# The diagonal of the first ten units summed by the tensor engine, and the weight work of a recurrent-attention kernel re-placed

## The chip, the cores and the metric

The kernel runs on one core of one Trainium2 chip. The metric is the device time of one launch in microseconds (us); smaller is better. The engines are called by their short names: PE (tensor engine, with its weight loads as PEld), DVE (vector engine), ACT (scalar engine), POOL (GpSimd) and SP (which only issues DMAs here).

## The reference

Three stages follow each other, in fp32; sizes are B=4, H=8, S=768, D=48 for the first, D_FF=1024 for the second, E=4 experts of head size 64 for the third.

```python
# stage 1: a recurrence over time with a decay w and a "bonus" u for the current step
for t in range(S):
    kt, vt, rt, wt = (k[:, :, t], v[:, :, t], r[:, :, t], w[:, :, t])
    cur = np.einsum('bhd,bhe->bhde', u[None] * kt, vt)
    y[:, :, t] = np.einsum('bhd,bhde->bhe', rt, state + cur)
    state = wt[:, :, :, None] * state + np.einsum('bhd,bhe->bhde', kt, vt)
# stage 2: x (4, 768, 384) -> relu(x @ w_in) -> conv over 3 steps -> h * sigmoid(conv) @ w_out
# stage 3: four causal softmax attentions on the result, mixed by a top-2 gate, output (4, 768, 384)
```

Only stage 1 and the weights of stage 2 are touched here. In stage 1 the bonus gives each time step one number per head, the sum over the 48 channels of r * u * k; it stands on the diagonal of the matrix that multiplies v.

## The kernel before

**Units and slots.** Stage 1 is cut into 32 units: a batch, a half of the sequence (three chunks of 128 steps) and a pair of heads, 2 x 48 channels padded to 2 x 64 partitions. `slot(u)` is written out 33 times in program order, and each engine works through its own instructions in the order in which the slots issue them. A slot finishes unit u, prepares unit u + 1, puts out unit u - 1, and from slot 5 on also carries one or two "groups" of stage 2 (a group is 128 of the 1024 hidden channels over one half of one batch). The slots are told apart below by DVE's first scan in them (L205, tile `Dp`), so "slot 3" runs from the L205 of slot 3 to that of slot 4.

**One unit.** `scan_d` and `scan_f` (L205, L212) are running products of the decay along time, `K` and `Q` (L215, L220) multiply k and r with them. `trans` turns K's chunks with PE (L266) and copies them out with ACT (`KT`, L268); `scores` is K times Q (L252), `state` KT times v (L278). `bonus` multiplies r, k and u on POOL (L225, L226), in a layout with time on the partitions (`rn`, `kn` of the `rkv` load), `diag` sums that over channels on DVE (L231, tile `e`) and spreads it on the diagonals of `AT` with two affine selects on POOL (L234). `masked` copies the scores below the diagonal into AT (L258, DVE). `carry` folds the state into the running states `Ss` (L289, L292, DVE). `yout` multiplies AT and the states out (L306, L312), `rows` splits the result in a high and a low part (ACT L324, DVE L325). `check` tests the decay's range on ACT (L243).

**PSUM.** `trans`, `state` and `yout` take their results in turn from one pool of two buffers (`ps_m`, name "m"), so `trans` of a unit gets the buffer that `carry` of the unit before it has read (L289). The hidden tile `hs` of a group has one buffer, which the ACT copy `ht` (L354) frees.

**Weights.** The weights of stage 2 arrive as float64 and are rebuilt from their words in eight pieces of 128 x 768, in slots 2 to 9 before the change: `conv1_w` masks and shifts on DVE (L75, L76), makes the low part on ACT (L72) and adds on POOL (L77); for the four `win` pieces `conv2_w` then rounds on ACT (L173) and takes the remainder on POOL (L174). In slots 10 to 17 the eight pieces are loaded again and `check_w` tests them on ACT (L185, L186).

**Stage 2 in a slot.** `mlp1` (L350), the ACT copies `ht` and `ct` (L354, L358), `conv` on DVE (L369 and L371, or L373 and L374) with a tanh on ACT (`st`, L377), `gate` on DVE (L387), and four groups later `mlp2` (L400).

Of the kernel before, what the change touches and what calls it, by code (L numbers as in the profile page):

```python
# [23 lines left out]
C = 128  # L24
# [63 lines left out]
def phase1(tc, nc, a, x2, ident, stat, lim, top, right, left2):  # L88
# [88 lines left out]

# [214 lines left out]
    def mlp2(g):  # L392
# [9 lines left out]
        if f == NF - 1:  # L402
# [23 lines left out]
    def slot(u):  # L426

        ga = 2 * u - G0
        s1u, nxt = u < 2 * NU, u + 1 < 2 * NU
        for i, (z, n, m) in enumerate(WS):  # L430
            if u == z - 2:
                load_w(n, m)
        if s1u:
            trans(u)
        conv(ga - 1)
        if nxt:
            bonus(u + 1)
# [25 lines left out]
        for i, (z, n, m) in enumerate(WS):  # L463
            if u == z:
                (conv2_w if i < 8 else check_w)(n, m)
        if u == 1:
            conv_w()
        if u == 18:
            rawc.close()
        groups(ga + 1)  # L470
        if u + 3 < 2 * NU:
            load(u + 3)

    with tc.manual_schedule(engines=mine):
        bonus(0)
# [643 lines left out]
```

## Time and profile before

| what | value |
|---|---|
| median of 3 runs | 658.96 us (657.47 to 659.04) |
| the profiled execution, its own time | 659.13 us |
| its span | 657.4 us |
| PE, DVE, ACT, POOL busy in the span | 586.6, 517.6, 347.9, 183.2 us |

The span is what the profiler saw from the first to the last instruction; the other 1.7 us lie around it. "Busy" counts an instruction from start to end, and a DVE instruction that is held up after its start counts as busy as well. A row of the timeline gives start, duration, engine, line, operation, what it writes and reads, shapes, and in brackets how long the engine had been idle before it and who ended that. Several instructions of one kind in a row are drawn together (x3).

### The profile page before, as it was taken

To read this page: it belongs to the slowest core of one execution; us is meant where nothing else is said; L and a number is where in the kernel's file an instruction comes from. 1 tells how busy PE (TensorE), PEld (TensorE's weight loads), DVE (VectorE), ACT (ScalarE), POOL (GpSimd) and SP (SyncE) were. 2 spreads that over 40 slices of the span, in tenths; PEclk is the share of its full clock that TensorE was granted. 3 is DMA by queue.
4 is the path that set the end of the run, shared out by engine and by line. 5 is a ranking of instruction groups with operands and counts; after the bars stand their busy time and mean duration, and the time that the engine had idled before them with its cause. 6 is when DMAs were issued, how large, how long until landed. Compare 5 with 4: busy or idle time off the path is not lost.

```text
span 657.4 us, 11247 instructions
## 1 busy us (share of the span) xinstructions
PE 586.6 (89%) x3978; PEld 464.9 (71%) x3978; DVE 517.6 (79%) x1151; ACT 347.9 (53%) x819; POOL 183.2 (28%) x245
## 2 busy tenths in 40 slices
PE   2665689799999999999999999989997999799896
PEld 1553567577676777777777776968786987788754
DVE  6999999988888999999995643688765876776471
ACT  3233444566666545556355552666654665556452
POOL 6478444222222233224321710030002002102260
PEclk9957789989999999999999999999998999999999
DMA  8655445475774455454513652265036514442502
GB/s 315 214 162 208 171 151 178 147 230 179 219 215 135 126 165 158 133 169 134 160 59 96 173 139 67 85 170 144 25 90 175 145 37 128 126 98 84 133 1 77
DMA packets 34401, 92.39 MB, mean 141 GB/s; under 512 B 5024, under 2 KB 14368, under 8 KB 34336
## 3 DMA queue, kind: packets, MB, share of 16 engines
q1 hardware_dynamic: 34336, 91.59, 46.7%
q8 instruction: 33, 0.54, 0.3%
q14 instruction: 32, 0.26, 0.1%
HBM read 53.77 MB, written 9.44 MB: 96 GB/s over the span
## 4 chain that ended last, share of the span: by engine, by line
PE 48%; DVE 29%; ACT 9%; DMA 7%; issue 4%; SPq 2%; POOL 1%; ACTq 0%; DVEq 0%; POOLq 0%
PE x L400 9%; PE hs L350 7%; PE m L767 6%; PE st L841 5%; PE m L891 5%; PE t L875 4%; DVE Fp L212 4%; PE m L903 4%; PE m L797 3%; DVE Dp L205 3%; DMA x<-x 2%; DVE AT L258 2%; DVE wm L76 2%; DVE ct L374 2%; DVE ct L369 2%
## 5 line engine op out<-in xcount | busy, mean ns | idle before, releaser
L400 PE MATMUL x<-gt,wout 128*128 128x386 f32 (+1 forms) x384 | 135.0, 490 | 0.0
L350 PE MATMUL hs<-X,win 128*128 128x384 f32 (+1 forms) x576 | 121.7, 357 | 8.2 <-ACT ht L354 8.1
L350 PEld LDWEIGHTS hs<-X,win 128*128 128x128 f32 x576 | 101.1, 193 | 17.6 <-ACT ht L354 11.7
L377 ACT ACTIVATE st<-ct 128x382 f32<-128x382 f32 (+1 forms) x64 | 33.6, 525 | 126.3 <-DVE ct L371 67.4
L400 PEld LDWEIGHTS x<-gt,wout 128*128 128x128 f32 x384 | 73.0, 192 | 35.8 <-issue 1.2
L855 ACT ACTIVATE A<-sm,mn 128x128 f32<-128x128 f32 (+5 forms) x96 | 63.8, 665 | 28.3 <-DVE mn L854 27.5
L854 DVE CUSTOM_DVE_ANT_0 sm<-st,mask 128x128 f32<-128x128 f32 (+5 forms) x96 | 58.3, 619 | 20.8 <-PE st L841 18.2
L234 POOL TENSOR_SCALAR_AFFINE_SELECT AT<-e 128x384 f32<-128x384 f32 x64 | 32.4, 531 | 141.8 <-DVE e L231 134.2
L875 PE MATMUL t<-ident,A 128*128 128x128 f32 x336 | 53.5, 276 | 2.1 <-ACT T L879 1.2
L266 PE MATMUL m<-ident,K 128*128 128x128 f32 x80 | 16.6, 312 | 36.6 <-DVE Ss L289 26.4
L841 PE MATMUL st<-sk,sq 128*128 128x384 f32 (+3 forms) x128 | 44.8, 360 | 2.7 <-DVE mn L854 1.8
L753 POOL TENSOR_TENSOR xs<-x,xs 128x768 fp32r<-128x768 f32 x12 | 22.4, 1884 | 88.8 <-ACT xs L752 88.8
L881 DVE COPY T<-t 128x128 f32<-128x128 f32 (+3 forms) x64 | 32.2, 504 | 18.4 <-PE t L875 17.9
L387 DVE SCALAR_TENSOR_TENSOR gt<-st,ht 128x382 f32<-128x382 f32 (+1 forms) x64 | 38.1, 596 | 10.9 <-ACT st L377 7.9
L841 PE MATMUL st<-sl,sq 128*128 128x384 f32 (+3 forms) x128 | 41.1, 334 | 5.8 <-DMA sl<-kl 5.8
L875 PEld LDWEIGHTS t<-ident,A 128*128 128x128 f32 x336 | 40.3, 140 | 8.4 <-issue 2.2
L252 PEld LDWEIGHTS sc<-Q,K 64*128 64x128 f32 x384 | 30.7, 218 | 20.5 <-issue 5.6
L266 PEld LDWEIGHTS m<-ident,K 128*128 128x128 f32 x80 | 11.0, 156 | 46.8 <-DVE Ss L289 29.8
L891 PE MATMUL m<-T,V 128*64 128x384 f32 (+2 forms) x288 | 43.8, 422 | 0.0
L879 ACT ACTIVATE T<-t 128x512 f32<-128x512 f32 (+3 forms) x64 | 28.6, 447 | 25.4 <-PE t L875 20.6
L252 PE MATMUL sc<-Q,K 64*128 64x128 f32 x384 | 37.6, 325 | 4.2 <-DVE AT L258 4.2
L358 ACT ACTIVATE ct<-ht,cwk 128x382 f32<-128x382 f32 (+1 forms) x64 | 39.5, 617 | 2.0
(126 smaller groups left out, 1216.2 us busy)
## 6 DMA issues: line engine op xcount, KB each, us to landing
wkr<-in_wkr SPq DMA_DIRECT2D x32, 578.0 KB, 3.8
rkv<-in_rkv SPq DMA_DIRECT2D x32, 480.0 KB, 4.5
rawt<-in_win SPq DMA_DIRECT2D x8, 768.0 KB, 5.5
rawt<-in_wout SPq DMA_DIRECT2D x8, 768.0 KB, 5.2
sk<-kh SPq DMA_DIRECT2D x32, 192.0 KB, 3.3
sl<-kl SPq DMA_DIRECT2D x32, 192.0 KB, 4.0
x<-x SPq DMA_DIRECT2D x12, 384.0 KB, 3.9
out_dram<-ot SPq DMA_DIRECT2D x24, 192.0 KB, 1.9
```

The lines of the kernel that those rows point to most:

```text
L252: nc.tensor.matmul(sc[j][:, c], t["K"][p, c], t["Q"][p, c], start=True, stop=True)
L350: nc.tensor.matmul(hs[:, 0:N], win[wi][:, f // 2, i, (f % 2) * 128:(f % 2 + 1) * 128], x[:, i, xi], start=(n == 0), stop=(n == 8))
L358: nc.scalar.activation(ct, ht[:, o:o + N], AF.Copy, scale=w[:, 1, f:f + 1])
L377: nc.scalar.activation(st, ct, AF.Tanh)
L387: nc.vector.scalar_tensor_tensor(gt, st, 1.0, ht[:, o:o + N], op0=OP.add, op1=OP.mult)
L400: nc.tensor.matmul(acc[0][i][:, 0:N], wout[:, f, i * 128:(i + 1) * 128], gt, start=(f == 0), stop=(f == NF - 1))
L767: nc.tensor.matmul(pt[:, 0:HT], w[wi][:, i, p * 128:(p + 1) * 128], xs[xi][:, i, s], start=(m == 0), stop=(m == 8))
L841: nc.tensor.matmul(st[:, z, 0:n], q[:, qi * C:(qi + 1) * C], k[:, z * n:(z + 1) * n], start=(i == 0), stop=(i == 1))
L854: nc.vector.tensor_tensor_reduce(o3, i3, m3, 1.0, 3e38, op0=OP.add, op1=OP.min, accum_out=mn)
L855: nc.scalar.activation(at, o3, AF.Exp, bias=mn, scale=-1.0, accum_out=rs[:, qi % 3:qi % 3 + 1])
L875: nc.tensor.transpose(pt[:, ki - k0], at[:, ki * C:(ki + 1) * C], self.ident)
L891: nc.tensor.matmul(po[o, lo:HT], V[:, ki, (2 * p + j) * 64:(2 * p + j + 1) * 64], Ts[j][:, ki, lo:], start=(ki == 0), stop=(ki == n - 1))
```

## The change

For units 0 to 9 (`BONUS_ON_PE = 10`) the two POOL products and the DVE sum go. DVE multiplies k by r in place, in the layout with channels on the partitions (`diag`, a 128 x 384 product), and in the next slot's `trans` PE multiplies each of the three chunks with a 2-column matrix `u_c`, which holds u of the pair of heads and zeros; ACT copies the 128 x 6 result to `e`, and the affine selects follow there. The r and k of these units in the other layout are no longer loaded (192 instead of 480 KB). `u_c` is loaded by two DMAs of single 4-byte elements, ahead of the loads of units 1 and 2.

The weight work is placed anew: the pieces are loaded one slot before their use, `conv1_w` stands at the end of slots 1 to 8, ahead of `masked`, and `conv2_w` at the head of the slot after, with its subtraction on DVE instead of POOL. `check` goes from behind the second conv to behind the first group, `check_w` from the slot's end to ahead of `scores`, `carry` from ahead of `masked` to behind `rows`, and the small `conv_w` from slot 1 to slot 0.

```diff
+        zn = 2 * CH * 64 if u < BONUS_ON_PE else NRKV
+        nc.sync.dma_start(z[:, 0:zn], a["rkv"][q, h][:, 0:zn])
+    u_c = cst.tile([128, HP, 2], F32, name="u_c")
+    nc.gpsimd.memset(u_c, 0.0)
+    for j in range(2):
+        nc.sync.dma_start(u_c[64 * j:64 * j + D, :, j],
+                          bass.AP(tensor=a["u"].tensor, offset=a["u"].offset + j * D, ap=[[1, D], [2 * D, HP]]))
...
-        nc.gpsimd.tensor_tensor(d1, t, _f(d0), op=OP.subtract)
+        nc.vector.tensor_tensor(d1, t, _f(d0), op=OP.subtract)
...
     def diag(u):
         t = T[u]
-        e = wk.tile([128, 2, CH], F32, name="e")
+        if u < BONUS_ON_PE:
+            nc.vector.tensor_tensor(t["k"], t["k"], t["r"], op=OP.mult)
+            return
+        e = t["e"] = wk.tile([128, 2, CH], F32, name="e")
         nc.vector.tensor_reduce(e, t["rn"], axis=AX.X, op=OP.add)
+        blocks(u)
...
+        if u < BONUS_ON_PE:
+            es = m[:, CH * 128:].rearrange("p (j c) -> p j c", j=2)
+            for c in range(CH):
+                nc.tensor.matmul(es[:, :, c], t["k"][:, c], u_c[:, hp], start=True, stop=True)
+            e = t["e"] = wk.tile([128, 2, CH], F32, name="e")
+            nc.scalar.activation(e, es, AF.Copy)
+            blocks(u)
         nc.scalar.activation(KT[:, 0:n], kt[:, 0:n], AF.Copy)
...
         if nxt:
-            bonus(u + 1)
+            if u + 1 >= BONUS_ON_PE:
+                bonus(u + 1)
             scan_d(u + 1)
-        for i, (z, n, m) in enumerate(WS[0:8]):
-            if u == z:
-                conv1_w(n, m)
+        for z, n, m in WS:
+            if u == z + 1:
+                conv2_w(n, m)
         gate(ga - 1)
         groups(ga)
+        if s1u:
+            check(u)
...
         gate(ga)
+        for z, n, m in WC2:
+            if u == z:
+                check_w(n, m)
         if s1u:
-            check(u)
             scores(u)
             state(u)
...
             diag(u + 1)
+        for z, n, m in WS:
+            if u == z:
+                conv1_w(n, m)
         if s1u:
-            carry(u)
             masked(u)
         if 0 < u <= 2 * NU:
             rows(u - 1)
-        for i, (z, n, m) in enumerate(WS):
-            if u == z:
-                (conv2_w if i < 8 else check_w)(n, m)
-        if u == 1:
+        if s1u:
+            carry(u)
+        if u == 0:
             conv_w()
```

In the changed file the lines stand 8 to 23 further down, so the scan `Dp` is L213 there, and so on. The order of DVE's instructions in slot 3 was this (`wm` is the rebuilt weight piece, `wkr` the load with w, k and r):

```order
L205 SCALAR_TENSOR_TENSOR Dp<-wkr,cD 128x387
L75 TENSOR_SCALAR wm<-rawt 128x768
L76 SCALAR_TENSOR_TENSOR wm<-rawt,wm 128x768
L210 RECIPROCAL cF<-Dp 128x3
L212 SCALAR_TENSOR_TENSOR Fp<-wkr,cF 128x387
L215 TENSOR_TENSOR K<-wkr,Fp 128x384
L220 TENSOR_TENSOR Q<-wkr,Dp 128x384
L231 TENSOR_REDUCE e<-rkv 128x6
L289 TENSOR_TENSOR Ss_128<-m,Dp 128x3x48
L292 SCALAR_TENSOR_TENSOR Ss_128<-Ss_128,Dp 128x48 x2
L258 COPY_PREDICATED AT<-msk,sc 128x384 x2
L325 TENSOR_TENSOR Y<-m,Y 128x384
```

The same slot on DVE after the change, with `win_143` the remainder of the piece before:

```order
L213 SCALAR_TENSOR_TENSOR Dp<-wkr,cD 128x387
L182 TENSOR_TENSOR win_143<-wm,win_142 128x768
L218 RECIPROCAL cF<-Dp 128x3
L220 SCALAR_TENSOR_TENSOR Fp<-wkr,cF 128x387
L223 TENSOR_TENSOR K<-wkr,Fp 128x384
L228 TENSOR_TENSOR Q<-wkr,Dp 128x384
L239 TENSOR_TENSOR wkr<-wkr 128x384
L76 TENSOR_SCALAR wm<-rawt 128x768
L77 SCALAR_TENSOR_TENSOR wm<-rawt,wm 128x768
L273 COPY_PREDICATED AT<-msk,sc 128x384 x2
L348 TENSOR_TENSOR Y<-m,Y 128x384
L312 TENSOR_TENSOR Ss_132<-m,Dp 128x3x48
```

The mask and shift (L75, L76, after: L76, L77) moved behind the products, the carry behind the output's split, and the remainder came in from POOL behind the first scan. On PE, slots 2 and 3 read before, with `sc` the scores:

```order
L266 MATMUL m<-ident,K 128x128 x3
L252 MATMUL sc<-Q,K 128x128 x6
L278 MATMUL m<-rkv,KT 64x48 x6
L306 MATMUL m<-AT,rkv 64x128 x6
L312 MATMUL m<-Q,Ss_124 64x128 x4
L266 MATMUL m<-ident,K 128x128 x3
L252 MATMUL sc<-Q,K 128x128 x6
L278 MATMUL m<-rkv,KT 64x48 x6
```

and now:

```order
L282 MATMUL m<-ident,K 128x128 x3
L287 MATMUL m<-u_c,wkr 128x2 x3
L267 MATMUL sc<-Q,K 128x128 x6
L301 MATMUL m<-rkv,KT 64x48 x6
L329 MATMUL m<-AT,rkv 64x128 x6
L335 MATMUL m<-Q,Ss_128 64x128 x4
L282 MATMUL m<-ident,K 128x128 x3
L287 MATMUL m<-u_c,wkr 128x2 x3
```

Three small products per unit stand between the transposes and the scores. On ACT, slot 13 (one of the eight with a weight check) read before, from the copy of KT on:

```order
L268 ACTIVATE KT<-m 128x256
L377 ACTIVATE st<-ct 128x386
L354 ACTIVATE ht<-hs 128x388
L358 ACTIVATE ct<-ht,cwk 128x386
L377 ACTIVATE st<-ct 128x386
L243 ACTIVATE Fp,stat<-wkr,lim 128x3x128 x2
L324 ACTIVATE Y<-m 128x384
L185 ACTIVATE rawt<-rawt 128x768
L186 ACTIVATE rawt,stat<-rawt,lim 128x768
L354 ACTIVATE ht<-hs 128x384
L358 ACTIVATE ct<-ht,cwk 128x382
```

and in the changed kernel:

```order
L291 ACTIVATE KT<-m 128x256
L400 ACTIVATE st<-ct 128x386
L377 ACTIVATE ht<-hs 128x388
L381 ACTIVATE ct<-ht,cwk 128x386
L258 ACTIVATE Fp,stat<-wkr,lim 128x3x128 x2
L400 ACTIVATE st<-ct 128x386
L193 ACTIVATE rawt<-rawt 128x768
L194 ACTIVATE rawt,stat<-rawt,lim 128x768
L347 ACTIVATE Y<-m 128x384
L377 ACTIVATE ht<-hs 128x384
L381 ACTIVATE ct<-ht,cwk 128x382
```

The decay's check went ahead of the second tanh, and the weight check ahead of the output copy `Y`.

## Rows read from the trace of the kernel before

**Rows 1.** Busy time by stretch: slots 1-9, 10-17, 18-28; clock, DMA share, GB/s.

```profile
16.70:122.30 105.60, 75.01 (x544) 58.42 (x545) 102.47 (x157) 41.23 (x90) 56.59 (x59) 0.81 0.55 179
122.30:211.70 89.40, 84.04 (x611) 63.27 (x610) 76.89 (x145) 58.42 (x126) 22.85 (x41) 0.98 0.64 193
211.70:324.40 112.70, 112.53 (x840) 85.75 (x839) 109.13 (x200) 59.88 (x141) 35.26 (x55) 1.00 0.48 150
```

**Rows 2.** Timeline of DVE and POOL in slot 3.

```profile
34.72 0.95 DVE L205 TENSOR_TENSOR_SCAN Dp<-wkr,cD 128x387 f32<-128x387 f32 x1
...
36.15 2.46 DVE L76 SCALAR_TENSOR_TENSOR wm<-rawt,wm 128x768 int32<-128x768 int32 x1
...
40.62 2.11 POOL L77 TENSOR_TENSOR wm<-wm,wy 128x768 int32<-128x768 int32 x1
41.00 2.15 DVE L220 TENSOR_TENSOR Q<-wkr,Dp 128x384 f32<-128x384 f32 x1
...
45.96 0.95 DVE L205 TENSOR_TENSOR_SCAN Dp<-wkr,cD 128x387 f32<-128x387 f32 x1
```

**Rows 3.** DVE by line, slots 1 to 9: count, busy us, mean ns, idle before.

```profile
L212 DVE TENSOR_TENSOR_SCAN Fp<-wkr,cF 128x387 f32<-128x387 f32 x9 | 15.5, 1726 | 0.4
L76 DVE SCALAR_TENSOR_TENSOR wm<-rawt,wm 128x768 int32<-128x768 int32 x8 | 12.2, 1519 | 0.3
...
L220 DVE TENSOR_TENSOR Q<-wkr,Dp 128x384 f32<-128x384 f32 x9 | 9.8, 1084 | 0.0
...
L215 DVE TENSOR_TENSOR K<-wkr,Fp 128x384 f32<-128x384 f32 x9 | 7.7, 853 | 0.3
...
L231 DVE TENSOR_REDUCE e<-rkv 128x6 f32<-128x288 f32 x9 | 4.0, 443 | 0.0
```

**Rows 4.** Three DVE lines over the whole run: shortest/median/longest in ns.

```profile
L76 DVE SCALAR_TENSOR_TENSOR wm<-rawt,wm x8: 957/959/2458, 27.4 to 110.8; 128x768 int32<-128x768 int32 x8
L212 DVE TENSOR_TENSOR_SCAN Fp<-wkr,cF x32: 964/965/2412, 6.0 to 336.2; 128x387 f32<-128x387 f32 x32
L215 DVE TENSOR_TENSOR K<-wkr,Fp x32: 557/559/1977, 7.5 to 337.2; 128x384 f32<-128x384 f32 x32
```

**Rows 5.** Timeline of POOL and DVE in slot 6.

```profile
80.52 1.83 POOL L174 TENSOR_TENSOR win<-wm,win 128x768 fp32r<-128x768 f32 x1 [0.38 <-ACT win L173]
80.93 0.55 DVE L325 TENSOR_TENSOR Y<-m,Y 128x384 fp32r<-128x384 f32 x1
```

**Rows 6.** Timeline of PE and ACT, slots 2 and 3.

```profile
32.54 0.90 PE L266 MATMUL m<-ident,K 128*128 128x128 f32 x3 [5.17 <-DVE Ss L289]
33.48 0.49 ACT L268 ACTIVATE KT<-m 128x384 f32<-128x384 f32 x1 [1.58 <-PE m L266]
33.95 2.11 PE L252 MATMUL sc<-Q,K 64*128 64x128 f32 x12 [0.50 <-DVE AT L258]
42.76 0.84 ACT L173 ACTIVATE win<-wm 128x768 fp32r<-128x768 f32 x1 [3.00 <-POOL wm L77]
```

**Rows 7.** Timeline of ACT, PE and DVE, slot 13.

```profile
161.70 0.60 ACT L243 ACTIVATE Fp<-wkr,lim 128x384 f32<-128x384 f32 x1
163.04 0.47 ACT L324 ACTIVATE Y<-m 128x384 fp32r<-128x384 f32 x1
...
165.35 0.48 ACT L354 ACTIVATE ht<-hs 128x384 f32<-128x384 f32 x1
...
165.89 1.83 PE L350 MATMUL hs<-X,win 128*128 128x384 f32 x9 [0.76 <-ACT ht L354]
...
166.52 0.78 DVE L369 SCALAR_TENSOR_TENSOR ct<-ht,cwk,ct 128x381 f32<-128x381 f32 x1 [1.23 <-ACT ct L358]
```

**Rows 8.** DMA issues of the first 30 us: KB each, us from issue to landing.

```profile
u_b<-in_u SPq DMA_DIRECT2D x1, 192.0 KB, 6.5
```

**Rows 9.** Timeline of DVE and PE, slot 19.

```profile
228.04 0.30 DVE L289 TENSOR_TENSOR Ss<-m,Dp 128x144 f32<-128x144 f32 x1
229.17 1.06 DVE L258 COPY_PREDICATED AT<-msk,sc 128x384 f32<-128x384 uint32 x2
...
229.55 0.38 PE L266 MATMUL m<-ident,K 128*128 128x128 f32 x2
230.12 0.54 DVE L325 TENSOR_TENSOR Y<-m,Y 128x384 fp32r<-128x384 f32 x1
```

More of the change, by code (lines that the diff above doesn't have):

```diff
@@ L43 @@
 SCALED_ON_POOL = 13
+BONUS_ON_PE = 10
 def _f(ap):
@@ L115, in load @@
         z = ld.tile([128, NRKV], F32, name="rkv")
-        nc.sync.dma_start(z, a["rkv"][q, h])
+        zn = 2 * CH * 64 if u < BONUS_ON_PE else NRKV
+        nc.sync.dma_start(z[:, 0:zn], a["rkv"][q, h][:, 0:zn])
         w, k, r = x[:, 0:NW + 1], x[:, NW + 1:NW + 1 + HT], x[:, NW + 1 + HT:]
@@ L229, in diag, with blocks @@
         t = T[u]
-        e = wk.tile([128, 2, CH], F32, name="e")
+        if u < BONUS_ON_PE:
+            nc.vector.tensor_tensor(t["k"], t["k"], t["r"], op=OP.mult)
+            return
+        e = t["e"] = wk.tile([128, 2, CH], F32, name="e")
         nc.vector.tensor_reduce(e, t["rn"], axis=AX.X, op=OP.add)
+        blocks(u)
+    def blocks(u):
+        t = T[u]
         AT = t["AT"] = wk.tile([128, 2, CH, C], F32, name="AT")
         for j in range(2):
-            nc.gpsimd.affine_select(AT[:, j], e[:, j][:, :, None].to_broadcast([128, CH, C]),
+            nc.gpsimd.affine_select(AT[:, j], t["e"][:, j][:, :, None].to_broadcast([128, CH, C]),
                                     pattern=[[0, CH], [1, C]], compare_op=OP.is_equal, fill=0.0, base=0,
@@ L263, in trans @@
         n = CH - h
-        kt = ps_m.tile([128, CH, 128], F32, name="m")
+        m = ps_m.tile([128, CH * 128 + 2 * CH], F32, name="m")
+        kt = m[:, 0:CH * 128].rearrange("p (c t) -> p c t", c=CH)
         for c in range(n):
@@ L415, in phase1 @@
     mine = {mine.PE, mine.DVE, mine.Activation, mine.Pool}
-    WS = ((2, "win", 0), (3, "win", 1), (4, "win", 2), (5, "wout", 0), (6, "win", 3), (7, "wout", 1), (8, "wout", 2),
-          (9, "wout", 3)) + tuple((10 + i, ("win", "wout")[i % 2], i // 2) for i in range(8))
+    WS = ((1, "win", 0), (2, "win", 1), (3, "win", 2), (4, "wout", 0), (5, "win", 3), (6, "wout", 1), (7, "wout", 2),
+          (8, "wout", 3))
+    WC2 = tuple((10 + i, ("win", "wout")[i % 2], i // 2) for i in range(8))
     def groups(g, last=False):
@@ L429, in slot @@
         s1u, nxt = u < 2 * NU, u + 1 < 2 * NU
-        for i, (z, n, m) in enumerate(WS):
-            if u == z - 2:
+        for z, n, m in WS + WC2:
+            if u == z - 1:
                 load_w(n, m)
@@ L462, in slot @@
             rows(u - 1)
-        for i, (z, n, m) in enumerate(WS):
-            if u == z:
-                (conv2_w if i < 8 else check_w)(n, m)
-        if u == 1:
+        if s1u:
+            carry(u)
+        if u == 0:
             conv_w()
@@ L474, in phase1 @@
     with tc.manual_schedule(engines=mine):
-        bonus(0)
         scan_d(0)
```

## The prediction, made before the changed kernel was run

> **What bounds the kernel now.** I read the busy times by stretch first, then DVE's lines in the first stretch, then single slots. The three stretches have different limits [rows 1]. In slots 1 to 9 DVE is busy for 102.47 of 105.6 us, PE for 75.01, at a mean granted clock of 0.81, so partly at 1.2 instead of 2.4 GHz: DVE sets the pace, 105.6 / 9 = 11.73 us a slot. In slots 18 to 28 PE is busy for 112.53 of 112.7 us, 10.25 a slot: that is what PE needs for a slot with two groups at full clock, and no slot with two groups can go much below it. In slots 10 to 17 neither is full (PE 84.04, DVE 76.89 of 89.4 us), and a slot takes 11.17.
>
> What DVE is busy with in slots 1 to 9 is partly waiting. Slot 3 runs from 34.72 to 45.96, 11.24 us [rows 2]. In it Q (L220) takes 2.15 us while POOL adds up a weight piece (L77, 40.62 to 42.73); it starts in that addition and ends 0.42 after it. L76 takes 2.46. Undisturbed, products of this shape take 0.557 (L215) and L76 0.957 [rows 4]. So a DVE instruction that reads two operands from SBUF waits for a POOL product to end. One that has an operand in PSUM does not: the output split (L325) takes 0.55 beside POOL's L174 [rows 5]. This agrees with the Trainium skill, SBUF — State Buffer, Who interferes with whom: a DVE instruction with two SBUF inputs contends with a GpSimd instruction that reads SBUF, and whoever comes second waits to the end of the first.
>
> In slots 10 to 17 a ring of ACT and DVE is what is late. In slot 13 ACT runs the decay check from 161.70 and the output copy Y at 163.04, then the weight check, and comes to the next hidden tile only at 165.35 [rows 7]. For that PE has stood idle 0.76 us (its next L350 needs the one `hs` buffer) and DVE 1.23 (its next conv needs `ct`).
>
> **What the change removes in slots 1 to 9.** The bonus products and the remainder (L225, L226, L174) leave POOL, and the addition (L77) moves beside `masked`, the split and the first carry instruction, which all have an operand in PSUM. What DVE lost to POOL, by its mean against its shortest time [rows 3, 4]: L212 (1.726 - 0.964) x 9 = 6.9; L76 (1.519 - 0.957) x 8 = 4.5; L220 (1.084 - 0.557) x 9 = 4.7; L215 (0.853 - 0.557) x 9 = 2.7. Together 18.8 us. I leave out what the scan L205 and the carries lose, because the affine selects, now at the slot's head, and the end of L77 will still hold such instructions up. L77 lasts 2.11 us [rows 2]; the two masked copies (1.06 together [rows 9]), the split (0.54) and the first carry (0.30) cover 1.9 of that. If that cover were gone, each of the eight would cost what Q lost in slot 3, 2.15 - 0.56 = 1.6, 12.8 in all.
>
> **What it adds there.**
> The remainder on DVE: four products of 768 columns, at L76's undisturbed 0.957, 3.8 us.
> The product k * r (0.557) for the sum over channels (0.443 [rows 3]): 9 x 0.11 = 1.0.
> A new wait ahead of the remainder. DVE comes to it right behind the first scan, but it needs the rounded piece from ACT, and ACT's queue has `e` and KT in front of that. Those wait for the transposes, and the transposes for the carry, which now ends a slot: the transposes have waited for L289 before too [rows 6]. From the end of the first carry instruction: transposes 0.90, the three sums, the copy `e`, KT 0.49, rounding 0.84 [rows 6]. The sums are not in this trace. Each of the 12 pieces of the scores costs 2.11 / 12 = 0.18 with 128 columns moving [rows 6]; the sums are 6 such pieces with 2 columns, so between nothing and 1.05, and I take 0.65. For `e` and the hand-overs I take 0.4, an estimate between nothing and KT's 0.49 for each. That makes 3.3 us, while DVE has the other two carries and the scan, 1.9. So DVE stands 1.4 in slots 2, 3 and 4, and some 0.6 in slot 6, where a conv lies between: 4.8 in all, from nothing (each part at its lower end, PE at full clock) to 8. Behind the remainder in DVE's queue stands the whole slot.
> The first hidden tile. DVE will reach the first conv sooner than PE and ACT deliver it: yout, L350 and two ACT copies now come behind a DVE that is two slots' gains ahead. I take 1.5, from 0.5 to 2.4.
> PE as floor. Slot 9 loses the weight piece and would take DVE 10.2; PE needs 10.25 and some 0.4 for the sums: 0.5 lost. Slots 7 and 8 stay with DVE, near 11.7.
> Sum for slots 1 to 9: 18.8 - 3.8 - 1.0 - 4.8 - 1.5 - 0.5 = 7.2 us gained. `conv_w` and one weight piece only change slots, which gives and takes the same.
>
> **Slots 10 to 17.** `check` (163.04 - 161.70 = 1.34 us of ACT) now runs where ACT waits for the conv anyhow, so the next hidden tile comes 1.3 us earlier. That is more than the 0.76 and the 1.23 that PE and DVE lost. PE becomes the limit at 10.25, and I add 0.15, because Y now stands behind the weight check and the carry behind Y: 8 x (11.17 - 10.40) = 6.2 us gained. At most it is 8 x 0.92 = 7.4, at least nothing.
>
> **Elsewhere.** The first ten units load 288 KB less each; at a DMA share of 0.55 in slots 1 to 9 [rows 1] no DVE wait hangs on it, so nothing. The two loads of `u_c` stand in SP's queue ahead of units 1 and 2. `u_b` took 6.5 us to land, queue included [rows 8]: so their cost lies between nothing (the 288 KB saved ahead of them outweigh it) and 6.5; I take nothing, since their bytes are few. From slot 18 on PE is full before and after, and only its order against the carry changes (rival below). The attention stage is untouched and comes earlier by what was won.
>
> **Sum.** 659.1 (the profiled execution, 0.2 above the median of 658.96) - 7.2 - 6.2 = 645.7 us.
>
> **The rivals.**
> *The early gain is eaten.* With PE at 1.2 GHz for much of slots 1 to 8, the ring carry, transposes, sums, scores, state, yout, split, carry takes nearly a slot, and the wait before the remainder grows to its upper end. For it: the clock of 0.81, and the carry behind the split is a new link. Against it: PE idles 30 us of that stretch. Time: 659.1 - 6.2 = 652.9.
> *The late gain is missing,* since PE waits for the carry in place of the hidden tile. Time: 659.1 - 7.2 = 651.9.
> *The new waits don't come,* as PE holds its full clock earlier: 4.8 and 1.5 come back, 639.4.
> *The loads of `u_c` hold up the first units,* at their upper bound: 645.7 + 6.5 = 652.2. By the Trainium skill, DMA: Bandwidth & Descriptors, a strided last dimension lowers to one descriptor per element, and pieces under 512 B are done as read-modify-write; no run so far shows such a load.
> *Slower.* One mechanism: carry behind masked and split, in every slot from 10 on. In slot 19 L289 ended at 228.34 and the next transposes began at 229.55, 1.21 later [rows 9]. Now two masked copies and a split, 1.06 + 0.54 less their overlap, about 1.4, come before it, so it is some 0.2 too late for PE. If each of 22 slots lost that, 4.4 would go: 650.1, still faster. It turns the sign only from 13.4 / 22 = 0.6 a slot on. Against it: DVE's ring back to the carry is shorter than PE's 10.25, so one late transpose should shift PE's phase once.
> *It does nothing,* if L77 loses its cover (12.8 back): 658.5.
>
> **How the numbers follow.** The forecast has a chance of 0.54, with a range of its own from 641 to 650. Early gain eaten 0.15, late gain missing 0.12, waits absent 0.10, `u_c` 0.03, no effect 0.03, slower 0.03. The range 639 to 652.5 holds the forecast, most of the waits' case and about half of the two at 652 and 653, some 0.8. What a measurement can tell from no change is 0.3%, 2 us: faster (below 657) is all but the last two cases, 0.94; same 0.03; slower 0.03.
>
> **What would show it.** Right: in slots 7 and 8 L212, L76, Q and K near their shortest times; DVE idle ahead of the remainder for about 1.4 in slots 2 to 4; slot 10 beginning near 115 instead of 122.3; slots 10 to 17 at 10.4 with no L350 waiting for `ht`; slots 18 to 28 unchanged at 10.25. Wrong: L77 still stretching DVE; transposes that wait for L289 (there L312) in late slots; the first scan of unit 1 starting later than before; PE's clock below 0.8 up to slot 9.

## The result, and the profile after

The changed kernel takes 642.75 us (median of four runs, 640.7 to 643.64) beside 659.0 us for the kernel before on the same chip: ratio 0.9752, interval 0.9724 to 0.9781. Run again later beside the kernel before (f1 below) it took 643.11 against 660.98, ratio 0.9729, 0.9695 to 0.9764. The forecast of 645.7 was 3 us too high; the range held the time.

The profiled execution of the changed kernel took 640.7 us (span 639.0), so it is set against the 659.1 us of the profiled execution before: 18.4 us less. The busy times by stretch (us, then PE, PEld, DVE, ACT, POOL; clock, DMA share, GB/s) answer to [rows 1]; slots are counted by DVE's first scan, now L213:

```profile
17.00:110.00 93.00, 73.34 (x572) 60.28 (x571) 85.44 (x155) 42.35 (x98) 32.31 (x40) 0.83 0.58 180
110.00:193.90 83.90, 82.02 (x610) 60.97 (x610) 77.83 (x146) 58.83 (x126) 22.49 (x38) 1.00 0.62 201
193.90:305.40 111.50, 111.50 (x839) 85.23 (x838) 107.82 (x199) 61.66 (x141) 36.74 (x57) 1.00 0.50 153
```

Slots 1 to 9 take 93.0 us instead of 105.6, 12.6 less (forecast 7.2). Slots 10 to 17 take 83.9 instead of 89.4, 5.5 less (forecast 6.2). Part of the 12.6 is only moved: `conv_w`, 1.5 us of DVE and a wait of 0.6 us for POOL in slot 1 before, now stands in slot 0, and slot 1 begins at 17.0 us instead of 16.7. Counted to the start of slot 10, where that cancels, the gain is 122.3 - 110.0 = 12.3 us. Slots 18 to 28 take 111.5 instead of 112.7, and PE is busy in all of it, as before. From the start of slot 29 to the end, nearly all of it the untouched attention stage, the kernel takes 333.0 us before and 333.5 after. In f1, the same program, it took 337.0. So this part alone moves by 4 us between executions, and differences of 1 to 3 us between kernels are better read from the stretches than from the whole time.

In the first stretch DVE's busy time fell by 102.47 - 85.44 = 17.0, and its idle time grew from 3.1 to 7.6, 4.4 more. DVE by line in that stretch (count, busy us, mean ns, idle before) answers to [rows 3]:

```profile
L213 DVE TENSOR_TENSOR_SCAN Dp<-wkr,cD 128x387 f32<-128x387 f32 x9 | 9.5, 1061 | 0.0
...
L220 DVE TENSOR_TENSOR_SCAN Fp<-wkr,cF 128x387 f32<-128x387 f32 x9 | 9.2, 1020 | 0.4
L77 DVE SCALAR_TENSOR_TENSOR wm<-rawt,wm 128x768 int32<-128x768 int32 x8 | 7.7, 960 | 0.3
L315 DVE SCALAR_TENSOR_TENSOR Ss<-Ss,Dp 128x48 f32<-128x48 f32 x18 | 6.0, 331 | 0.6
...
L228 DVE TENSOR_TENSOR Q<-wkr,Dp 128x384 f32<-128x384 f32 x9 | 5.3, 586 | 0.0
...
L223 DVE TENSOR_TENSOR K<-wkr,Fp 128x384 f32<-128x384 f32 x9 | 5.2, 573 | 0.3
L392 DVE SCALAR_TENSOR_TENSOR ct<-ht,cwk,ct 128x381 f32<-128x381 f32 x8 | 4.9, 612 | 0.9 <-ACT ct L381 0.9
...
L239 DVE TENSOR_TENSOR wkr<-wkr 128x384 f32<-128x384 f32 x8 | 4.4, 551 | 0.0
L182 DVE TENSOR_TENSOR win<-wm,win 128x768 fp32r<-128x768 f32 x4 | 3.8, 958 | 4.2 <-ACT win L181 4.1
```

The lines are those of before, moved down (those of the weight work by one): L220 is the second scan (L212 before), L77 DVE's second integer step on a weight piece (L76 before), L228 is Q (L220), L223 is K (L215), L315 the carries, L392 the first conv, L239 the new k * r and L182 the remainder. The four lines of [rows 3] that POOL had held stand within 0.06 us of their shortest times of [rows 4], where they had been 0.30 to 0.76 above. The last row is the remainder on DVE with the new wait: 4.2 us of idle time ahead of it, nearly all of it for ACT's rounded piece.

Two things more are read from the timeline of slots 1 to 3 (start us, us, engine, line):

```profile
24.39 1.27 PE L287 MATMUL m<-u_c,wkr 128*128 128x2 f32 x6
25.70 0.18 ACT L289 ACTIVATE e<-m 128x6 f32<-128x6 f32 x1 [5.51 <-PE m L287]
26.14 0.84 ACT L181 ACTIVATE win<-wm 128x768 fp32r<-128x768 f32 x1
27.02 0.96 DVE L182 TENSOR_TENSOR win<-wm,win 128x768 fp32r<-128x768 f32 x1 [1.57 <-ACT win L181]
...
31.98 1.04 DVE L273 COPY_PREDICATED AT<-msk,sc 128x384 f32<-128x384 uint32 x2
32.21 1.81 POOL L78 TENSOR_TENSOR wm<-wm,wy 128x768 int32<-128x768 int32 x1 [5.27 <-DVE wm L77]
32.92 0.54 DVE L348 TENSOR_TENSOR Y<-m,Y 128x384 fp32r<-128x384 f32 x1
```

The chain sums on PE, copy `e`, rounding, remainder stands there in the order forecast: sums 1.27, `e` 0.18, rounding 0.84, and DVE idle 1.57 before the remainder. And POOL's addition (L78) runs beside the masked copies (L273) and the split (L348) without stretching them; it needs 1.81 us itself, against 2.11 in slot 3 before [rows 2].

In slots 10 to 17 before, PE's waits for `ht` were these (us in total, times, longest):

```profile
PE hs L350 <- ACT ht L354: 5.4, 7, 2.1
```

In the changed kernel no product L373 (before L350) stands among the waits for `ht` there. Over the whole run, by the page's costliest groups, only 0.8 us of that is left:

```profile
L373 PE MATMUL hs<-X,win 128*128 128x384 f32 (+1 forms) x576 | 119.2, 352 | 0.8 <-ACT ht L377 0.8
```

What the transposes (L282) wait for there now is the split, by the view of waits (us in total, times, longest), and not for long:

```profile
PEld m L282 <- DVE Y L348: 6.6, 8, 1.1
```

### The profile page after: what moved, and what is told of

The parts are those of the page before. It is cut to its first block, busy times and chain, and to the rows that moved or that the text cites. A ratio compares the mean times of both kernels' runs of the same rounds, so it can differ in the third digit from the quotient of the medians.

```text
span 639.0 us, 11367 instructions
## 1 busy us (share of the span) xinstructions
PE 590.0 (92%) x4038; PEld 471.0 (74%) x4038; DVE 499.5 (78%) x1155; ACT 351.7 (55%) x829; POOL 155.7 (24%) x222
## 4 chain that ended last, share of the span: by engine, by line
PE 61%; DVE 18%; DMA 8%; ACT 6%; issue 3%; POOL 1%; SPq 1%; DVEq 0%; ACTq 0%; POOLq 0%
PE x L423 12%; PE hs L373 10%; PE m L796 7%; PE m L920 5%; PE st L870 5%; PE t L904 4%; PE m L932 4%; PE m L826 3%; DMA wkr<-in_wkr 3%; PE sc L267 3%; PE m L329 2%; PE m L335 2%; DVE sm L883 2%; DVE Fp L220 1%; DVE AT L273 1%
## 5 line engine op out<-in xcount | busy, mean ns | idle before, releaser
L423 PE MATMUL x<-gt,wout 128*128 128x386 f32 (+1 forms) x384 | 133.5, 485 | 0.0
L373 PE MATMUL hs<-X,win 128*128 128x384 f32 (+1 forms) x576 | 119.2, 352 | 0.8 <-ACT ht L377 0.8
L373 PEld LDWEIGHTS hs<-X,win 128*128 128x128 f32 x576 | 99.5, 190 | 7.0 <-issue 4.3
L249 POOL TENSOR_SCALAR_AFFINE_SELECT AT<-e 128x384 f32<-128x384 f32 x64 | 35.8, 583 | 133.9 <-DVE e L242 112.9
L410 DVE SCALAR_TENSOR_TENSOR gt<-st,ht 128x382 f32<-128x382 f32 (+1 forms) x64 | 41.1, 642 | 10.8 <-ACT st L400 7.7
L377 ACT ACTIVATE ht<-hs 128x384 f32<-128x384 f32 (+1 forms) x64 | 30.9, 483 | 25.1 <-PE hs L373 25.1
L282 PE MATMUL m<-ident,K 128*128 128x128 f32 x80 | 16.7, 312 | 29.5 <-DVE Y L348 21.5
L282 PEld LDWEIGHTS m<-ident,K 128*128 128x128 f32 x80 | 10.1, 153 | 42.2 <-DVE Y L348 30.7
L213 DVE TENSOR_TENSOR_SCAN Dp<-wkr,cD 128x387 f32<-128x387 f32 x32 | 36.4, 1136 | 5.5 <-DMA wkr<-in_wkr 5.5
```

Source lines behind the costliest of these rows:

```text
L213: nc.vector.tensor_tensor_scan(fl(t["Dp"]), t["w"][:, 0:NW], fl(cD), 0.0, op0=OP.mult, op1=OP.add)
L249: nc.gpsimd.affine_select(AT[:, j], t["e"][:, j][:, :, None].to_broadcast([128, CH, C]), pattern=[[0, CH], [1, C]], compare_op=OP.is_equal ...
L373: nc.tensor.matmul(hs[:, 0:N], win[wi][:, f // 2, i, (f % 2) * 128:(f % 2 + 1) * 128], x[:, i, xi], start=(n == 0), stop=(n == 8))
L410: nc.vector.scalar_tensor_tensor(gt, st, 1.0, ht[:, o:o + N], op0=OP.add, op1=OP.mult)
L423: nc.tensor.matmul(acc[0][i][:, 0:N], wout[:, f, i * 128:(i + 1) * 128], gt, start=(f == 0), stop=(f == NF - 1))
```

## The experiments

**Theory before them.** DVE in slots 1 to 9 was slow because POOL's products held it up, and it is fast because the bonus products left POOL and the addition found cover; from slot 10 on the place of `check` alone makes the gain. **Rivals.** For the early slots: the order of the weight work is enough, and the bonus on TensorE matters little. For the late slots: the lead that the early slots hand over, or the new place of the weight check, makes the gain.

Each ratio is to the kernel before on the same chip (660.06 us in the first four runs, 661.05 in the next four, 660.98 in the last).

### e1: the bonus back on POOL

```diff
-BONUS_ON_PE = 10
+BONUS_ON_PE = 0
+        bonus(0)
         scan_d(0)
```

> The changed kernel with the bonus of units 0 to 9 back on POOL and its load back to 480 KB; the new order is kept. If the early gain comes from DVE no longer being held up by POOL's products, the twenty products at 0.8 to 1.0 us each hold DVE again, some 0.9 us in each of nine slots: 642.8 + 8 = 651 (647 to 655), and in slots 1 to 9 the scans and products on DVE are again well over their shortest times. Rival: the early gain comes from the new order of the weight work and the carry; then the time stays within 2 us of 642.8.

Measured: 645.01 us, ratio 0.9767 (0.9735 to 0.98), below my theory's range and 0.2 us beyond the rival's; slots 1 to 9 in 95.1, slots 10 to 17 in 85.4. My theory fell: the early gain is nearly all there with the bonus on POOL. DVE by line in slots 1 to 9 of this kernel:

```profile
L315 DVE SCALAR_TENSOR_TENSOR Ss<-Ss,Dp 128x48 f32<-128x48 f32 x18 | 11.8, 654 | 0.6
...
L77 DVE SCALAR_TENSOR_TENSOR wm<-rawt,wm 128x768 int32<-128x768 int32 x8 | 9.2, 1153 | 0.3
...
L182 DVE TENSOR_TENSOR win<-wm,win 128x768 fp32r<-128x768 f32 x4 | 5.4, 1352 | 0.5 <-ACT win L181 0.5
```

and the timeline around the end of a slot, of POOL and then of DVE:

```profile
45.58 0.79 POOL L233 TENSOR_TENSOR rkv<-rkv 128x288 f32<-128x288 f32 x1
46.45 1.46 POOL L234 TENSOR_TENSOR rkv<-rkv,u_b 128x288 f32<-128x288 f32 x1
...
44.98 1.47 DVE L315 SCALAR_TENSOR_TENSOR Ss<-Ss,Dp 128x48 f32<-128x48 f32 x2
46.36 0.95 DVE L213 TENSOR_TENSOR_SCAN Dp<-wkr,cD 128x387 f32<-128x387 f32 x1
47.24 1.49 DVE L182 TENSOR_TENSOR win<-wm,win 128x768 fp32r<-128x768 f32 x1
```

The bonus still holds DVE up, but at the slot's end: the carries cost 11.8 - 6.0 = 5.8 us more than in the changed kernel, L77 1.5, the remainder 1.6. In return the wait ahead of the remainder is nearly gone (0.5 instead of 4.2), ACT's queue no longer having the sums in front of the rounding, and the sum over channels costs 4.0 against 4.4 for k * r. In all DVE is busy for 92.1 us of the stretch, 6.7 more than in the changed kernel, and idle for 2.9, 4.6 less. So of the 6.7 us that TensorE's diagonal saves DVE in these slots, 4.6 come back as idle time.

### e2: the diagonal on TensorE alone

The kernel before with `u_c`, the smaller load, the new `diag` and the new `trans`; the order and the remainder's engine are those of before.

```diff
+BONUS_ON_PE = 10
-            bonus(u + 1)
+            if u + 1 >= BONUS_ON_PE:
+                bonus(u + 1)
...
-        bonus(0)
```

> The kernel before with only the diagonal of units 0 to 9 moved to PE (and the smaller load); the order of the weight work, the checks and the carry is that of before. If POOL's bonus products held DVE up, it gains what they held, some 5 us (the remainder and the addition on POOL still hold DVE): 654 (651 to 656). Rival, the order makes the gain: 659 within 2 us. In slots 10 to 17 the ring of ACT stays, 11.2 us a slot, in either case.

Measured: 653.87 us, ratio 0.9916 (0.9887 to 0.9944); slots 1 to 9 in 101.5, slot 1 starting at 15.1 instead of 16.7 and slot 10 at 116.5, 5.7 earlier than before; slots 10 to 17 in 88.9, as long as before. DVE by line in slots 1 to 9:

```profile
L219 DVE TENSOR_TENSOR_SCAN Fp<-wkr,cF 128x387 f32<-128x387 f32 x9 | 15.0, 1665 | 0.4
L77 DVE SCALAR_TENSOR_TENSOR wm<-rawt,wm 128x768 int32<-128x768 int32 x8 | 12.2, 1521 | 0.3
...
L227 DVE TENSOR_TENSOR Q<-wkr,Dp 128x384 f32<-128x384 f32 x9 | 9.7, 1083 | 0.0
...
L314 DVE SCALAR_TENSOR_TENSOR Ss<-Ss,Dp 128x48 f32<-128x48 f32 x18 | 5.1, 286 | 0.6
```

This shows whose work held which line. The second scan, L77 and Q are as slow as in [rows 3] (there L212, L76 and L220: 1726, 1519, 1084 ns) though no bonus product is on POOL: they were held by the weight work there. The bonus had held other lines, the carries above all (L314: 286 ns, where L292 before has 432). The smaller load comes with this edit; no wait of DVE for a DMA stands in slots 1 to 9 of this run or of the kernel before.

### f2: the order of the weight work alone

The changed kernel with the bonus on POOL as in e1, and `check` and `check_w` where they stood before.

```diff
-BONUS_ON_PE = 10
+BONUS_ON_PE = 0
...
         groups(ga)
-        if s1u:
-            check(u)
...
         gate(ga)
-        for z, n, m in WC2: ... check_w(n, m)
         if s1u:
+            check(u)
             scores(u)
...
             carry(u)
+        for z, n, m in WC2: ... check_w(n, m)
```

> The new places of the weight work (addition behind the diagonal, remainder on DVE behind the next slot's first scan, carry at the slot's end, first convolution weights in slot 0) without the other two parts: GpSimd forms and DVE sums the products of every unit, and check and check_w stand where they stood before. Theory A (the place of GpSimd's addition made the early gain): slots 1 to 9 in 95 us against 105.6 before, slots 10 to 17 unchanged at 89, ratio 0.984. Theory B (the bonus's products on GpSimd made it, and the good time of the kernel that keeps them came from its other edits in some way not yet seen): slots 1 to 9 above 100 us, ratio 0.99 or more.

Measured: 650.77 us, ratio 0.9839 (0.9801 to 0.9878); slots 1 to 9 in 95.6, slots 10 to 17 in 87.7. Theory A as forecast. The stretch of slots 1 to 9, then DVE by line in its early slots:

```profile
18.60:114.20 95.60, 66.96 (x521) 52.27 (x520) 92.67 (x155) 41.41 (x90) 51.35 (x54) 0.84 0.63 196
```

```profile
L220 DVE TENSOR_TENSOR_SCAN Fp<-wkr,cF 128x387 f32<-128x387 f32 x9 | 9.3, 1036 | 0.4
L77 DVE SCALAR_TENSOR_TENSOR wm<-rawt,wm 128x768 int32<-128x768 int32 x8 | 9.2, 1152 | 0.3
...
L228 DVE TENSOR_TENSOR Q<-wkr,Dp 128x384 f32<-128x384 f32 x9 | 4.9, 550 | 0.0
```

The same lines that stayed slow in e2 are fast here, L77 nearly so, with the bonus still on POOL. Of the 12.6 us in slots 1 to 9, the order alone gives 105.6 - 95.6 = 10.0. Some 2 of these are `conv_w`, which moved to slot 0 (slot 1 starts at 18.6 here); slot 10 starts at 114.2, 8.0 us earlier than before, against 5.7 for the diagonal alone and 12.3 for both.

### e6: the addition without its cover

```diff
+        for z, n, m in WS: if u == z: conv1_w(n, m)   (slot's head, behind conv2_w)
         gate(ga - 1)
...
-        for z, n, m in WS: if u == z: conv1_w(n, m)   (ahead of masked)
```

> The changed kernel with mask, shift and addition of the eight weight pieces back at the head of the slot, behind the remainder. If it is the cover of masked, split and first carry that makes POOL's addition cheap, each addition again holds the scan or a product behind it, about 1.2 to 1.6 each: 642.8 + 11 = 654 (650 to 657). Rival, the place makes no difference as POOL would be waited for in one place or another: within 2 us.

Measured: 651.89 us, ratio 0.9866 (0.984 to 0.9892); slots 1 to 9 in 102.3. DVE by line in slots 1 to 9, and one place of the timeline:

```profile
L220 DVE TENSOR_TENSOR_SCAN Fp<-wkr,cF 128x387 f32<-128x387 f32 x9 | 15.0, 1670 | 0.4
L223 DVE TENSOR_TENSOR K<-wkr,Fp 128x384 f32<-128x384 f32 x9 | 11.1, 1235 | 0.3
```

```profile
42.10 2.50 POOL L78 TENSOR_TENSOR wm<-wm,wy 128x768 int32<-128x768 int32 x1 [2.67 <-DVE cF L218]
...
43.04 1.98 DVE L223 TENSOR_TENSOR K<-wkr,Fp 128x384 f32<-128x384 f32 x1
```

The second scan and K are held for (15.0 - 9.2) + (11.1 - 5.2) = 11.7 us, beside the forecast's bound of 12.8, and the stretch grows by 9.3. K starts in the addition and ends at 45.02, 0.42 after it: the same 0.42 as Q in [rows 2]. POOL pays too: 2.50 us here, 1.81 under cover.

### e3: the remainder back on POOL

```diff
-        nc.vector.tensor_tensor(d1, t, _f(d0), op=OP.subtract)
+        nc.gpsimd.tensor_tensor(d1, t, _f(d0), op=OP.subtract)
```

> The changed kernel with the remainder of the four win pieces back on POOL. DVE loses four products (3.8 us) and its three waits for the rounded piece (4.1), and is held again by four POOL products of 2 us, some 1.5 each (6): net 642.8 - 2 = 641 (639 to 644). Rival, the move of the remainder to DVE is a main part of the gain: 647 or more.

Measured: 642.62 us, ratio 0.9715 (0.9686 to 0.9744); slots 1 to 9 in 93.9 (93.0 and 93.4 in the changed kernel). The engine of four remainders makes no difference that I can measure, and the rival falls.

### e7: the carry ahead of the addition

```diff
+        if s1u:
+            carry(u)
         for z, n, m in WS:
...
-        if s1u:
-            carry(u)
         if u == 0:
```

> The changed kernel with the carry put ahead of the weight piece and of masked. The transposes of the next unit are then free some 3 us earlier, so DVE's wait for the rounded piece (4.1 us) goes: 642.8 - 4 = 639 (637 to 641). Rival, that wait is covered by the next one behind it, PE or ACT: 642.8 within 1.5 us. If the late carry cost PE something in slots 10 to 31, more than 4 us come back.

Measured: 642.17 us, ratio 0.9706 (0.9681 to 0.9731), outside the forecast and at the rival's time. The wait ahead of the remainder does go, but slots 1 to 9 shrink only to 91.9, by 1.1 to 1.5 and not by the wait's 4.1. The view by line and the timeline of slots 2 and 3 show what came instead:

```profile
L213 DVE TENSOR_TENSOR_SCAN Dp<-wkr,cD 128x387 f32<-128x387 f32 x10 | 13.5, 1349 | 0.0
...
L392 DVE SCALAR_TENSOR_TENSOR ct<-ht,cwk,ct 128x381 f32<-128x381 f32 x8 | 6.7, 838 | 0.0
...
L182 DVE TENSOR_TENSOR win<-wm,win 128x768 fp32r<-128x768 f32 x4 | 4.5, 1125 | 0.4
```

```profile
33.10 1.47 DVE L213 TENSOR_TENSOR_SCAN Dp<-wkr,cD 128x387 f32<-128x387 f32 x1
...
31.93 1.82 POOL L78 TENSOR_TENSOR wm<-wm,wy 128x768 int32<-128x768 int32 x1 [4.78 <-DVE wm L77]
```

The carries were part of the addition's cover. Without them DVE comes to the first scan while the addition still runs (to 33.75), and the scan takes 1.47 instead of 0.96; by their means the first scan loses 9 x 0.29 = 2.6 us, the first conv 8 x 0.23 = 1.8, the remainder 4 x 0.17 = 0.7. DVE's idle time in the stretch falls by 4.7 us (7.6 to 2.9) and its busy time rises by 3.6 (85.4 to 89.0): most of the wait was exchanged for contention, which is neither the theory nor the rival. Slots 18 to 28 take 115.0 by DVE's scans (111.5 in the changed kernel).

### e4: `check` back behind the gate

```diff
         groups(ga)
-        if s1u:
-            check(u)
...
         gate(ga)
+        if s1u:
+            check(u)
         for z, n, m in WC2:
```

> The changed kernel with the decay check put back behind the second conv and gate, ahead of the weight check. If that check on ACT in front of the next hidden tile made slots 10 to 17 long, they go back from 10.5 to 11.2 and the time to 642.8 + 5.5 = 648.3 (646.5 to 650). Rival, the move of the weight check made the late gain: no change, within 1.5 us.

Measured: 650.3 us, ratio 0.9845 (0.9817 to 0.9873), just above the forecast's range. The rival falls. The first stretch keeps its gain (92.6), the second takes 93.4 us, 9.5 more than in the changed kernel and 4 more than before, and here `check` and the weight check both stand ahead of the copy Y. DVE waits for that copy 13.6 us in the stretch, where it was 3.4 in the changed kernel:

```profile
DVE Y L348 <- ACT Y L347: 13.6, 8, 1.8
```

### f3: `check` moved in the kernel before

```diff
         groups(ga)
+        if s1u:
+            check(u)
...
         if s1u:
-            check(u)
             scores(u)
```

> The kernel before with check(u) alone moved up behind groups(ga). Theory A (the late gain is ACT's order alone): slots 10 to 17 in 83 to 85 us against 89.4, slots 1 to 9 at 104 to 106, ratio 0.991 (0.989 to 0.993). Rival (the late gain needs the 12 us lead that the early slots of the changed kernel hand over, or the weight work's other place in slots 10 to 17): slots 10 to 17 above 87, ratio 0.996 or more.

Measured: 656.68 us, ratio 0.9929 (0.9898 to 0.9959). By stretch:

```profile
16.90:122.00 105.10, 70.00 (x545) 54.90 (x545) 101.98 (x157) 41.44 (x90) 56.52 (x59) 0.84 0.54 179
122.00:205.00 83.00, 81.34 (x609) 61.68 (x609) 80.32 (x145) 57.98 (x126) 26.23 (x41) 1.00 0.64 205
205.00:320.10 115.10, 114.57 (x845) 85.52 (x843) 111.42 (x200) 60.27 (x141) 36.59 (x56) 1.00 0.49 149
```

Slots 10 to 17 fall from 89.4 to 83.0 with this one edit and without any lead from the early slots, so the rival falls. Of these 6.4 us the whole time shows 4.3 (660.98 - 656.68): counted by DVE's scans, slots 18 to 28 take 115.1 instead of 112.7, with PE busy in 114.57 of them. That DVE had run ahead of PE and is held there till PE has caught up is how I read this; it was not tested.

### e5: `check_w` back at the slot's end

```diff
         gate(ga)
-        for z, n, m in WC2: ... check_w(n, m)
...
             carry(u)
+        for z, n, m in WC2: ... check_w(n, m)
```

> The changed kernel with the weight check put back to the slot's end, behind the output copy and the carry. My theory: on ACT it stands between the second tanh and the next hidden tile in either place, so the ring is as long as now: 642.8 within 1.5 us, if anything a little faster since the output copy is earlier. Rival, the move of the weight check made the late gain: 648.

Measured: 640.62 us, ratio 0.9707 (0.9679 to 0.9736); slots 10 to 17 in 82.1 instead of 83.9, with PE busy all the time. That is 2.2 us less than the changed kernel, more than the 1.5 allowed, and the other way from the rival. So the weight check ahead of Y costs 1.8 us in eight slots, 0.22 a slot; the prediction had put down 0.15 for it and the carry behind Y together.

### e8: all units' diagonals on TensorE

```diff
-BONUS_ON_PE = 10
+BONUS_ON_PE = 32
```

> The changed kernel with the diagonal of all 32 units on PE. If PE is the limit from slot 10 on, each of 22 slots gets longer by the sums, 0.4 to 0.7 us: 642.8 + 12 = 655 (651 to 658). Rival, DVE and its waits for POOL are the limit there too: then it gets faster, 640.

Measured: 655.83 us, ratio 0.9919 (0.9889 to 0.9949). Slots 18 to 28 take 119.0 us with PE busy throughout, (119.0 - 111.5) / 11 = 0.68 more a slot, near the 0.73 us that the six sums take at their fastest (below). Where PE sets the pace, this work can't be put on it.

### f1 and f4: the changed kernel again, and a combination

f1 is the changed kernel itself. f4 has `check_w` at the slot's end as e5, and the carry ahead of the addition as e7, but in slots 2 to 9 alone.

```diff
+        if s1u and 2 <= u <= 9:
+            carry(u)
         for z, n, m in WS: ... conv1_w(n, m)
...
-        if s1u:
+        if s1u and not 2 <= u <= 9:
             carry(u)
+        for z, n, m in WC2: ... check_w(n, m)
```

> The changed kernel itself, as the base for the three beside it on one chip. Both theories: 0.975 of the kernel before (0.972 to 0.978), slots 1 to 9 in 93 us, slots 10 to 17 in 84 us, slots 18 to 28 in 111.5 us.

> The changed kernel with check_w back at the slot's end and carry ahead of the addition in slots 2 to 9 alone. Theory A (DVE's order is the bound in slots 1 to 9, TensorE from slot 10): slots 1 to 9 in 92 us, slots 10 to 17 in 82 us, slots 18 to 28 at 111.5; 2 to 3 us less than the changed kernel on the same chip, ratio 0.971. Rival (TensorE's work is the floor everywhere past slot 6, and what DVE saves turns into a wait): the changed kernel's ratio within 1 us.

Measured: f1 643.11 us, 0.9729 (0.9695 to 0.9764), slots in 93.4, 84.9 and 111.7. f4 639.45 us (635.07 to 644.67), 0.9668 (0.9621 to 0.9714), slots in 92.65, 82.3 and 111.1.

f4 has the shortest median of all, 3.7 us under f1 on the same chip. The two intervals overlap a little, so I call it probably better, not shown. By the stretches it reaches slot 29 at 302.8 us, against 305.4 and 306.9 in the two profiles of the changed kernel, and the gain is that of slots 10 to 17; the first stretch gains little, for the reason that e7 shows. The rival is not ruled out for the end of that stretch: in slots 7 to 9 of the changed kernel PE is busy for 11.7, 11.2 and 11.4 of 12.2, 11.4 and 11.4 us, so little was to be won there.

## Why the prediction was right, point by point

**Held lines of DVE: right in size, unseparated in cause.** 18.8 us were to come back on four lines; by their means 17.8 did: second scan 9 x 0.706, integer step 8 x 0.559, Q 9 x 0.498, K 9 x 0.280. The prediction named the bonus, the remainder and the addition together as what held them. e2 and f2 separate them: for three of the four lines (second scan, integer step, Q) it was the weight work. Moving that alone brings slot 10 forward by 8.0 us (10.0 in slots 1 to 9, less what `conv_w` costs in slot 0), moving the bonus alone by 5.7 (105.6 - 101.5 = 4.1 in slots 1 to 9 and 1.6 ahead of slot 1). The forecast time itself does not test the part that gave the change its name: with the bonus still on POOL, e1 takes 645.01, nearer to the forecast of 645.7 than the changed kernel.

**What the sum left out: too low by 3.0.** DVE's busy time was to fall by 18.8 - 3.8 - 1.0 = 14.0 and fell by 17.0. The prediction put the first scan, the carries and the first conv at nothing, because POOL's remaining work would go on holding them. It holds them less than before. Their lines before, in the view of [rows 3]:

```profile
L205 DVE TENSOR_TENSOR_SCAN Dp<-wkr,cD 128x387 f32<-128x387 f32 x10 | 11.9, 1193 | 0.0
...
L292 DVE SCALAR_TENSOR_TENSOR Ss<-Ss,Dp 128x48 f32<-128x48 f32 x18 | 7.8, 432 | 0.6
...
L369 DVE SCALAR_TENSOR_TENSOR ct<-ht,cwk,ct 128x381 f32<-128x381 f32 x8 | 6.2, 769 | 0.0
```

By the means the carries fell to 331, 18 x 0.10 = 1.8; the first conv to 612, 8 x 0.16 = 1.3; the first scan, 1153 without slot 10's, which the view takes in, to 1061, 9 x 0.09 = 0.8. `conv_w`, which the prediction took as a mere change of slots, left the stretch with 1.5. The gate line L410, 649 ns where it had 552, takes 0.8 back, a conv line (L396, 1219 ns where it had 611) 0.6, and the four lines above gave 1.0 less than forecast: 1.8 + 1.3 + 0.8 + 1.5 - 0.8 - 0.6 - 1.0 = 3.0. The step that failed is this leaving out: a size, not the mechanism.

**The new waits: too high by 1.8.** They were to cost 4.8 + 1.5 + 0.5 = 6.8 and cost 5.0. Ahead of the remainder it was 4.1 in three slots (1.57 and 1.24 in the first two), where four waits of 1.4, 1.4, 1.4 and 0.6 had been put down; at the first conv 0.9, in two slots, instead of 1.5. PE as floor in slot 9 is there, PE being busy for all 11.4 us of it, but DVE stands idle for only 0.3; the slot takes 11.4 where some 10.7 had been put down. DVE's idle time grew by 4.4 and not by 5.0, since `conv_w` took its 0.6 along.

Two parts of that chain were wrong. The six sums took 1.27 us for an estimated 0.65, more than the prediction's upper bound of 1.05. And the transposes do not wait for the carry, where the prediction let the chain begin: they start at 23.70, right behind the split (23.10 to 23.64, L348) and while the first carry instruction (L312, 23.56 to 23.86) still runs. The view of waits for slots 1 to 9 names the split too:

```profile
PE m L282 <- DVE Y L348: 19.6, 7, 5.6
```

In program order the split now frees its PSUM buffer ahead of the carry, and that the transposes are given that buffer is how I read it. In e7, where the carry comes first again, they wait for the carry. From the start of `e` to the start of the rounding it was 0.44 us, where 0.4 for `e` and the hand-overs and 0.49 for KT had been put down; that took some back.

Of the 12.6 - 7.2 = 5.4 us by which slots 1 to 9 were forecast too long, 1.5 are thus lines left out, 1.8 waits, and 2.1 `conv_w`, which slot 0 pays.

**Slots 10 to 17: right.** 5.5 for 6.2, and f3 and e4 confirm that it is `check` on ACT. e5 shows where the rest lies: the weight check ahead of the copy Y. Without it there PE is busy for 81.98 of 82.0 us, which is the limit that the prediction named.

**Elsewhere: right.** The loads of `u_c` took 5.4 us to land, and unit 1's first scan began at 9.29 us instead of 9.74. Slots 18 to 28 did not grow, so the rival that makes it slower (a late carry at 0.2 a slot) is absent: PE is busy throughout, and the transposes follow the split and not the carry.

**The cover of the addition: right.** e6 takes it away and loses 9.3 us in slots 1 to 9, the second scan and K ending behind the addition. This agrees with the rule that the prediction cited from the Trainium skill, SBUF — State Buffer, Who interferes with whom.

**The parts do not add up as one might think.** Alone, the order saves 10.2 us of the whole time, `check` 4.3, the diagonal 660.06 x (1 - 0.9916) = 5.5, in all 20. Together they save 16 to 18. Order and `check` about add up: 14.5 apart, 660.06 x (1 - 0.9767) = 15.4 together in e1, which has the weight check's new place besides. The diagonal is what shrinks, from 5.5 to some 1 to 2.5 us (0.9767 against 0.9752 and 0.9729, with intervals that overlap). By e1's rows, in the new order the bonus still holds the carries, the integer step and the remainder, but its way over PE and ACT puts the remainder's rounding behind it, and two thirds of what DVE saves come back as idle time.

**Left open.** Why the part from slot 29 on takes 333 to 337 us in two executions of the same program was not tried, nor what the granted clock means for the early slots (below).

## What to carry to other kernels

When DVE and GpSimd both work on SBUF, put GpSimd's long products beside DVE instructions that read PSUM before taking them off GpSimd: here the place of the addition with its integer steps was worth 9.0 us to the start of slot 10 (e6, 119.0 against 110.0), moving the diagonal to another engine 5.7 (e2). Try a change's parts alone and all but one: here a part that saves 5.5 us alone is worth 1 to 2.5 beside the others. And follow what an operation pulls along in an in-order queue: the copy `e` itself is 0.18 us, but everything behind it in ACT's queue waited for its sums.

## What was not expected of the hardware

The six sums have two moving columns each, yet in slot 2 they take 1.27 us, 0.21 each. By the view of that line the 128 x 128 weights in f32 are loaded for each, and a load lasts about as long as the product (shortest, median and longest in ns):

```profile
L287 PEld LDWEIGHTS m<-u_c,wkr x60: 190/333/337, 8.7 to 97.2; 128*128 128x128 f32 x60
L287 PE MATMUL m<-u_c,wkr x60: 170/352/374, 8.7 to 97.2; 128*128 128x2 f32 x60
```

I read the weight load as what has to be costed with so few moving columns; no run changes the one without the other.

The sums also tell what the column of the granted clock can and can't say. Those of slot 4, begun at 43.49, took 1.28 us in a window that reads 0.50, and those begun at 60.66 took 0.73 at 1.00. But those of slot 2 took 1.27 in a window that reads 1.00 too (windows of 3 us around slot 2 and slot 4, then the timeline):

```profile
24.00:27.00 3.00, 3.00 (x21) 2.94 (x19) 1.41 (x3) 1.30 (x4) 1.33 (x4) 1.00 1.01 356
42.00:45.00 3.00, 1.99 (x10) 1.98 (x12) 2.71 (x7) 0.20 (x2) 1.67 (x2) 0.50 0.76 236
```

```profile
60.66 0.73 PE L287 MATMUL m<-u_c,wkr 128*128 128x2 f32 x6
```

The trace explains it: its entries of the clock begin only at 30.5 us, and a window before them reads 1.00 because no entry lowers it. From there on the sums and the clock agree in every slot: 1.26 to 1.28 us at 0.50 or 0.51, the lower level of 1.2 GHz (begun at 33.90, 43.49, 52.99 and 73.60), 0.73 at 1.00, 2.4 GHz (60.66, 85.37, 96.75). At the full clock they cost about what the prediction had put down. In f1, the same program, the entries begin at 18.5 us, and the sums of slot 2, begun at 24.34, took 1.28 us at 0.50. So the reading of 1.00 in slot 2 here shows no full clock, and mean clocks over slots 1 to 9 of two runs can't be compared: e4 reads 0.93 there against 0.83, but its entries begin at 48.6 us, and its sums before that took 1.28 all the same.
